# Dense groups of 512 tokens that run across batches, with a group of 256 between two halves of the first

## The chip, the core and the metric

The kernel runs on one core of one Trainium2 chip. The metric is device time in microseconds, the median of three runs. TensorE (PE in the profile) multiplies matrices, VectorE (DVE) and ScalarE (ACT) work elementwise, GpSimd (POOL) makes masks and indirect transfers, and SyncE (SP) issues the other transfers.

## The reference

Attention of 4 batches, 8 heads, 576 positions and 64 elements a head feeds a dense layer, and that a mixture of eight experts with one expert per token. `N` is 2304 tokens, `D` 512.

```python
# attention: heads 0-3 plain, heads 4-7 dilated
scores = (1.0 / np.sqrt(64)) * np.matmul(q, k.transpose(0, 1, 3, 2))
rel = pos[:, None] - pos[None, :]
mask_plain = (rel >= 0) & (rel < 32)
mask_dil = (rel >= 0) & (rel < 128) & (rel % 4 == 0)
attn = softmax(np.where(masks, scores, -1e9));  x = attn @ v       # -> [2304, 512]
# dense, w_in [512, 2048], w_out [2048, 512]
r = np.maximum(x @ w_in, 0.0)
y = (s * (r * r) + b) @ w_out
# experts, w1 [8, 512, 1024], w2 [8, 1024, 512]
logits = (y / |y|) @ (emb / |emb|).T / tau
e = argmax(logits);  gate = softmax(logits)[e]
out = gate * (np.maximum(y @ w1[e], 0.0) @ w2[e])
```

## The kernel before, in words

All products keep full precision with a split: each operand is a high part and a low part, and `mm3` (L273 to L275) issues three matmuls, high x high, low x high, high x low, into one PSUM bank.

**Attention** is cut into units of 192 tokens of one batch (`UT`, three units a batch, twelve in all), and each unit into four items of two heads: items 0 and 1 are plain heads, 2 and 3 dilated. An item has four steps: `attn_a` loads query and key (`qkp`, `qkd`) and values (`vp`, `vd`); `attn_b` makes scores on PE (`pS`, L129), adds the mask and takes the row minimum on DVE (L135, L138), exponentials on ACT (L140, one per window), and scales on DVE (L146); `attn_c` transposes on PE (`pT`, L154) and copies on ACT (`sT`, L159); `attn_d` multiplies with values (`po`, L173) and writes the high part of x on ACT (`xhi`, L181) and the low part on DVE (`xlo`, L182). The first unit of a batch has narrower first windows, which splits some of its DVE operations.

**Dense layer.** Tokens are taken in groups of 384 (`G`, six groups, two units each). A group walks over 16 chunks of 128 hidden columns. `gemm1` multiplies x by a chunk of `w_in` (12 matmuls into `ph`, one of two banks), then ReLU on ACT (`r`, L284), the square, and the high and low part `gh` and `gl`; in group 0 the square is on ACT (L288 to L291), later on DVE (L293 to L295). `gemm2`, two steps behind, multiplies by a chunk of `w_out` (9 matmuls into three banks `py0` to `py2`, which stand over the whole group). Behind the 16th chunk the banks are copied to `ysb` (L314), and routing takes norms and dots with the expert embeddings (L510, L513).

**Weights** come as 64 bit numbers. `weight_prep` loads 512 KB (`raw`) and makes the high and low part of a chunk: four DVE operations (L261, L264, L265, L269) and two on ACT (L263, L268). Two conversions serve one chunk, so there are 32.

**Order.** The startup runs the eight items of group 0 with eight conversions in between. Then the loop in `phase1` emits two slots a step, `gemm1` of one step and `gemm2` of the step two before; PE keeps just the order in which it is emitted, the other engines' instructions are ordered by a scheduler. The rest of attention is done in pairs of items and put into slots by `attn_steps`: loads 5 slots ahead, scores at the slot, transposes `TURN` = 4 slots later, outputs `PERIOD` = 6 slots later. Each of the first twelve steps also emits two conversions. In the last group, from step `EARLY` = 10 on, the experts' first units are set up (`experts_early`), with tables and gates made by small products.

**Experts.** Tokens are gathered by expert; units of 512 (pairs) and 256 (singles) tokens run `mm3` with weights split by ACT and DVE (L803, L804). The last group's routing transposes y on PE (`pyT`, L530) and makes the dots there (`pd`, L540).

Of the kernel before, what the change touches and what calls it, by code (L numbers as in the profile page):

```python
# [23 lines left out]
NTE = 15  # L24
NTT = 18

LOAD, TURN = -5, 4
LAG_FIRST = (0, 1, 4, 5)
PERIOD, START = 6, 2
LA = 2  # L30
EARLY = 10
# [3 lines left out]
P = 128  # L35
# [4 lines left out]
UT = 192  # L40
NU = NT // UT
G = 384
NG = NT // G
BIG = 1.0e9
QKP = 2 * UT + 2 * (UT + 32)
QKD = 4 * 64 + 4 * 80


class Kern:
    def __init__(self, tc, qkp, qkd, vp, vd, w_in, w_out, s, b, emb, tau, w1, w2, out):  # L50
        self.tc, self.nc = tc, tc.nc
        self.qkp, self.qkd, self.vp, self.vd = qkp, qkd, vp, vd
        self.w_in, self.w_out, self.s, self.b = w_in, w_out, s, b
        self.emb, self.tau, self.w1, self.w2, self.out = emb, tau, w1, w2, out
# [14 lines left out]
    def attn_consts(self, pool):  # L69
        nc = self.nc  # L70
        self.mask = pool.tile([P, 96], F32, name="mask")
        nc.gpsimd.memset(self.mask, 0.0)
        self.band(self.mask[0:64])
        self.band(self.mask[64:128])

    def load_plain(self, un):
        nc = self.nc
        ap = self.ppool if un == 0 else self.apool
        qk = ap.tile([P, QKP], F32, tag="qkp", name=f"qkp{un}", bufs=1)
        v = ap.tile([96, 3, 4, D], F32, tag="vp", name=f"vp{un}", bufs=1)  # L80
        nc.sync.dma_start(out=qk, in_=self.qkp[un])
        nc.sync.dma_start(out=v, in_=self.vp[un])
        return qk, v

    def load_dil(self, un, pr):
        nc = self.nc
        i = 2 * un + pr - 2
        ap = self.ppool if i < 2 else self.apool
        qk = ap.tile([P, QKD], F32, tag="qkd", name=f"qkd{i}", bufs=2)
        v = ap.tile([80, 2, 4, D], F32, tag="vd", name=f"vd{i}", bufs=2)  # L90
        nc.sync.dma_start(out=qk, in_=self.qkd[i])
        nc.sync.dma_start(out=v, in_=self.vd[i])
        return qk, v

    def attn_a(self, un, pr, ps):
        if (un, pr) in self.loaded:
            qk, vn = self.loaded.pop((un, pr))
        elif pr >= 2:
            qk, vn = self.load_dil(un, pr)
        else:  # L100
            if pr == 0:
                self.nat = self.load_plain(un)
            qk, vn = self.nat
        n = un % 3
        dil = pr >= 2
        if dil:
            qT, kT = qk[:, 0:256], qk[:, 256:576]
            wins = [(80 * t + 32, 48) if n == 0 else (80 * t, 80) for t in range(4)]
            groups = [(0, 4)]
        else:  # L110
            qT, kT = qk[:, UT * pr:UT * pr + UT], qk[:, 2 * UT + 224 * pr:2 * UT + 224 * pr + 224]
            wins = [(32, 64) if n == 0 and t == 0 else (64 * t, 96) for t in range(3)]
            groups = [(0, 1), (1, 3)] if n == 0 else [(0, 3)]
        hs = slice(0, 2) if dil else slice(2 * pr, 2 * pr + 2)
        return dict(un=un, pr=pr, u=f"{un}_{pr}", dil=dil, hs=hs, vn=vn, qT=qT, kT=kT, ps=ps,
                    wins=wins, groups=groups, ws=[w for _, w in wins])

    def attn_b(self, c):
        nc, ap, ps = self.nc, self.apool, c["ps"]
        u, qT, kT, ws, nb = c["u"], c["qT"], c["kT"], c["ws"], len(c["ws"])  # L120
        pS = ps.tile([P, 512], F32, tag="pa", name=f"pS{u}")
        extra = 4 * c["un"] + c["pr"] < 6
        prb = (self.ppool if extra else ap).tile([P, 4, 96], F32, tag="prob", name=f"prob{u}", bufs=6 if extra else 2)
        st = ap.tile([P, 16], F32, tag="st", name=f"st{u}", bufs=8)
        c["prb"] = prb
        for t, (k0, w) in enumerate(c["wins"]):
            for h in range(2):
                sl = slice(64 * h, 64 * h + 64)
                nc.tensor.matmul(pS[sl, 96 * t:96 * t + w], lhsT=qT[sl, 64 * t:64 * t + 64],  # L129
                                 rhs=kT[sl, k0:k0 + w], start=True, stop=True)  # L130
        full = 80 if c["dil"] else 96
        pS3 = pS[:, 0:384].rearrange("p (t w) -> p t w", t=4)
        for i, j in c["groups"]:
            w = ws[i]
            nc.vector.scalar_tensor_tensor(  # L135
                out=prb[:, i:j, :w], in0=pS3[:, i:j, :w], scalar=-0.125,
                in1=self.mask[:, full - w:full].unsqueeze(1).to_broadcast([P, j - i, w]), op0=ALU.mult, op1=ALU.add)
            nc.vector.tensor_reduce(out=st[:, i:j], in_=prb[:, i:j, :w], axis=AX.X, op=ALU.min)  # L138
        for t, w in enumerate(ws):
            nc.scalar.activation(prb[:, t, :w], prb[:, t, :w], AF.Exp, scale=-1.0,  # L140
                                 bias=st[:, t:t + 1], accum_out=st[:, 4 + t:5 + t])
        nc.vector.tensor_scalar_add(st[:, 8:8 + nb], st[:, 4:4 + nb], 1e-9)
        nc.vector.reciprocal(st[:, 12:12 + nb], st[:, 8:8 + nb])
        for i, j in c["groups"]:
            w = ws[i]
            nc.vector.tensor_mul(prb[:, i:j, :w], prb[:, i:j, :w],  # L146
                                 st[:, 12 + i:12 + j].unsqueeze(2).to_broadcast([P, j - i, w]))

    def attn_c(self, c):
        nc, ap, ps = self.nc, self.apool, c["ps"]  # L150
        u, ws, prb = c["u"], c["ws"], c["prb"]
        pT = ps.tile([P, 512], F32, tag="pa", name=f"pT{u}")
        for t, w in enumerate(ws):
            nc.tensor.transpose(pT[:w, P * t:P * t + P], prb[:, t, :w], self.ident)  # L154
        sT = ap.tile([P, 512], F32, tag="sT", name=f"sT{u}")
        cp = nc.scalar.copy
        cuts = [0, len(ws)] if ws[0] == ws[1] else [0, 1, len(ws)]
        for i, j in zip(cuts, cuts[1:]):
            cp(sT[:ws[i], P * i:P * j], pT[:ws[i], P * i:P * j])  # L159
        c["sT"] = sT  # L160

    def attn_d(self, cs):
        nc = self.nc
        c = cs[0]
        un, pr, dil, ws, k = c["un"], c["pr"], c["dil"], c["ws"], len(cs)
        po = c["ps"].tile([P, 512], F32, tag="pa", name=f"po{c['u']}")
        m = 48 if dil else 64
        for i, c in enumerate(cs):
            for t, w in enumerate(ws):
                for h in range(2):  # L170
                    lv = c["vn"][:w, h, t, :] if dil else c["vn"][:w, t, c["hs"].start + h, :]
                    o = UT * i + m * t
                    nc.tensor.matmul(po[64 * h:64 * h + 64, o:o + m], lhsT=lv,  # L173
                                     rhs=c["sT"][:w, P * t + 64 * h:P * t + 64 * h + m], start=True, stop=True)
        half, d0 = (un // 2) % 2, UT * (un % 2)
        hi, lo = (x[half][:, pr:pr + k, d0:d0 + UT] for x in (self.xhi, self.xlo))
# [27 lines left out]
    def attn_steps(self, n0, n1, ps):  # L204
# [4 lines left out]
        for j in range((n1 - n0) // 2):  # L209
            n = n0 + 2 * j  # L210
            t = 32 * (j // 4) + PERIOD * (j % 4) + START
# [14 lines left out]
            todo += [(t + LOAD, 0, n, a), (t, 2, n, b), (t + TURN, 3, n, c), (t + PERIOD, 1, n, d)]  # L226
# [3 lines left out]
    def weights_setup(self, left, right):  # L230
# [9 lines left out]
        self.x_half(right)  # L240

    def x_half(self, pool):
        i = len(self.xhi)
        self.xhi.append(pool.tile([P, 4, G], F32R, name=f"xhi{i}", bufs=1))
# [855 lines left out]
```

## Time and profile before

| | |
|---|---|
| median of 3 runs | 780.06 us (779.97 to 781.83) |
| profiled execution | 782.15 us, span 780.3 us |
| PE | 754.1 us busy, 97% of the span |
| DVE | 560.1 us, 72% |
| ACT | 393.9 us, 50% |
| POOL | 55.0 us, 7% |
| first dense matmul | at 37.44 us |

The span is the profiled part of that execution. Shares are means over stages that differ: attention and conversions alone at the start, the dense layer with attention beneath it up to 484.8 us, its end with the experts' setup up to 518 us, and the experts. Matmuls overlap each other, so the length shown for one is longer than its distance to the next; distances of starts tell what one costs.

### The profile page before, as it was taken

How to read it: one execution, taken by the hardware profiler on the slowest of the kernel's cores; microseconds unless marked ns; L12 is line 12 of the kernel's file. 1: busy time of each engine (PE TensorE's matmuls, PEld its weight loads, DVE VectorE, ACT ScalarE, POOL GpSimd, SP SyncE). 2: the span in 40 equal slices, each digit the busy share in tenths (PEclk: the TensorE clock that was granted, in tenths of full speed). 3: DMA queues.
4: the chain of work that ended last, by engine and by line, in shares of the span. 5: the costliest groups of instructions: out<-in, count | busy, mean ns of one | idle time of the engine just before them, and what ended most of it. 6: DMA issues, size and time to landing. Idle time of an engine off the chain costs nothing. (4 is left out here: it accounts for less than half of the span.)

```text
span 780.3 us, 14255 instructions
## 1 busy us (share of the span) xinstructions
PE 754.1 (97%) x5154; PEld 668.0 (86%) x5154; DVE 560.1 (72%) x1410; ACT 393.9 (50%) x925; POOL 55.0 (7%) x59
## 2 busy tenths in 40 slices
PE   5789999999999999999999999999999999999996
PEld 4578888988988888988888989898998989898895
DVE  5989996967476747764776578948666867768671
ACT  5778785534354436442644242642335655656550
POOL 1000000000000000000000000010422221211011
PEclk9999999999999999999999999999999999999999
DMA  7656664111121112110300010630236139887710
GB/s 259 217 205 209 196 202 161 57 40 60 40 73 39 48 34 91 40 47 18 109 18 1 1 42 1 216 95 15 82 108 203 43 108 308 260 302 229 262 48 25
DMA packets 33372, 88.04 MB, mean 113 GB/s; under 512 B 4294, under 2 KB 4294, under 8 KB 33168
## 3 DMA queue, kind: packets, MB, share of 16 engines
q1 hardware_dynamic: 29936, 76.84, 29.8%
q0 software_dynamic: 3360, 10.23, 4.0%
q8 instruction: 43, 0.70, 0.4%
q14 instruction: 33, 0.27, 0.1%
HBM read 94.39 MB, written 10.22 MB: 134 GB/s over the span
## 5 line engine op out<-in xcount | busy, mean ns | idle before, releaser
L804 DVE TENSOR_TENSOR wl<-raw,wh 128x1024 fp32r<-128x1024 f32 x96 | 113.6, 1221 | 29.4 <-ACT wh L803 29.4
L275 PE MATMUL ph<-xhi,wil 128*128 128x384 f32 x384 | 130.6, 340 | 1.1 <-DVE wil L269 1.1
L273 PE MATMUL ph<-xhi,wih 128*128 128x384 f32 x384 | 131.1, 341 | 0.4 <-ACT r L284 0.3
L274 PE MATMUL ph<-xlo,wih 128*128 128x384 f32 x384 | 130.2, 339 | 0.0
L273 PE MATMUL py<-woh,gh 128*128 128x512 f32 x288 | 118.0, 410 | 0.1
L275 PE MATMUL py<-woh,gl 128*128 128x512 f32 x288 | 114.2, 397 | 3.1 <-DVE gl L291 2.4
L274 PE MATMUL py<-wol,gh 128*128 128x512 f32 x288 | 113.6, 394 | 0.0
L284 ACT ACTIVATE r<-ph 128x384 f32<-128x384 f32 x96 | 46.9, 488 | 106.2 <-PE ph L275 102.6
L803 ACT CAST wh<-raw 128x1024 fp32r<-128x1024 f32 x96 | 96.1, 1054 | 5.1 <-DMA raw<-in_moe_w 5.1
L294 ACT ACTIVATE gh<-r,sb 128x384 fp32r<-128x384 f32 x80 | 49.1, 614 | 74.9 <-PE py L274 61.7
L295 DVE SCALAR_TENSOR_TENSOR gl<-r,sb,gh 128x384 fp32r<-128x384 f32 x80 | 49.3, 617 | 47.5 <-ACT gh L294 45.3
L513 DVE CUSTOM_DVE_ANT_0 junk<-ysb,enb 128x512 bf16<-128x512 f32 x120 | 82.4, 687 | 0.9
L273 PEld LDWEIGHTS ph<-xhi,wih 128*128 128x128 f32 x384 | 73.0, 190 | 4.9 <-ACT r L284 0.5
L274 PEld LDWEIGHTS ph<-xlo,wih 128*128 128x128 f32 x384 | 72.9, 190 | 4.0
L293 DVE SCALAR_TENSOR_TENSOR r<-r,sb 128x384 f32<-128x384 f32 x80 | 49.4, 617 | 35.5 <-ACT r L284 35.3
L275 PEld LDWEIGHTS ph<-xhi,wil 128*128 128x128 f32 x384 | 72.8, 190 | 2.0 <-DVE wil L269 2.0
L273 PE MATMUL ph<-xh,wh 128*128 128x256 f32 x256 | 73.5, 287 | 0.0
L274 PE MATMUL ph<-xl,wh 128*128 128x256 f32 x256 | 73.4, 287 | 0.0
L275 PE MATMUL ph<-xh,wl 128*128 128x256 f32 x256 | 73.1, 286 | 0.0
L140 ACT ACTIVATE prob<-prob,st 128x80 f32<-128x80 f32 (+3 forms) x168 | 58.4, 350 | 28.3 <-DVE st L138 28.3
L275 PEld LDWEIGHTS py<-woh,gl 128*128 128x128 f32 x288 | 54.2, 188 | 16.3 <-DVE gl L291 2.9
L273 PE MATMUL po<-wh,hh 128*128 128x512 f32 x168 | 66.8, 398 | 0.0
(256 smaller groups left out, 1350.7 us busy)
## 6 DMA issues: line engine op xcount, KB each, us to landing
raw<-in_moe_w SPq DMA_DIRECT2D x96, 512.0 KB
raw<-in_moe_w_in SPq DMA_DIRECT2D x16, 512.0 KB
raw<-in_moe_w_out SPq DMA_DIRECT2D x16, 512.0 KB
qkd<-in_qkd SPq DMA_DIRECT2D x24, 288.0 KB
qkp<-in_qkp SPq DMA_DIRECT2D x12, 416.0 KB
ydram<-ysb SPq DMA_DIRECT2D x18, 256.0 KB
vd<-in_vd SPq DMA_DIRECT2D x24, 160.0 KB
vp<-in_vp SPq DMA_DIRECT2D x12, 288.0 KB
```

The costliest lines, as they stand in the source:

```text
L140: nc.scalar.activation(prb[:, t, :w], prb[:, t, :w], AF.Exp, scale=-1.0, bias=st[:, t:t + 1], accum_out=st[:, 4 + t:5 + t])
L273: nc.tensor.matmul(out, lhsT=ah, rhs=bh, start=first, stop=False)
L274: nc.tensor.matmul(out, lhsT=ah, rhs=bl, start=False, stop=False)
L275: nc.tensor.matmul(out, lhsT=al, rhs=bh, start=False, stop=last)
L284: nc.scalar.activation(r, ph[:, :G], AF.Relu)
L293: nc.vector.scalar_tensor_tensor(out=r, in0=r, scalar=self.sb[:, 0:1], in1=r, op0=ALU.mult, op1=ALU.mult)
L294: nc.scalar.activation(gh, r, AF.Identity, bias=self.sb[:, 1:2])
L295: nc.vector.scalar_tensor_tensor(out=gl, in0=r, scalar=self.sb[:, 1:2], in1=gh.bitcast(F32), op0=ALU.add, op1=ALU.subtract)
L513: ins = nc.vector.tensor_tensor_reduce(out=self.junk, in0=y, in1=self.enb[:, e], scale=1.0, scalar=0.0, op0=ALU.mult, op1=ALU.add, accum_o ...
L803: nc.scalar.copy(h, r)
L804: nc.vector.tensor_sub(l, r, h.bitcast(F32))
```

## The change

Units become 256 tokens and run across batches: nine units, 36 items, always four windows of 96 keys, with extra masks (`EDGE`) where a batch begins inside a unit. Dense groups are 512, 256, 512, 512, 512 tokens (`GU` in units), and group 1, of 256, runs its 16 chunks between chunks 0 to 7 and chunks 8 to 15 of group 0 (`ORDER`, 80 steps). Group 0's four `py` banks stand all that time. In steps 10 to 25 (`SHARED`) group 1's two `py` banks are two of the four banks that `ph` and attention take in turn (`bank_a`); before and after that all four are in turn. In the last group `ph` has two banks of its own. Attention of each group has its own tempo. Of the 32 conversions four stand in the startup, then two a step up to 20, and six in seven steps from step 8 on. The loads of `s` and `b` stand behind those of the first unit, and the first unit's inputs lie in the buffer that later holds another half of x.

```diff
-LOAD, TURN = -5, 4
+LOAD = -5
-PERIOD, START = 6, 2
-EARLY = 10
+EARLY = 11
-UT = 192
+UT = 256
-G = 384
-NG = NT // G
+G = 512
+GU = (2, 1, 2, 2, 2)
+XH = (0, 1, 1, 0, 1)
+SEGS = [(0, 0, 8), (1, 0, 16), (0, 8, 16)] + [(g, 0, 16) for g in range(2, NG)]
+ORDER = [(g, f) for g, f0, f1 in SEGS for f in range(f0, f1)]
+TEMPO = [(2, 6, 4), (50, 3, 2), (66, 6, 4), (98, 6, 4)]
+EDGE = {0: 0, 2: 16, 4: 32, 6: 48, 7: -16}
+PRE = (0, 1, 4)
+NPREP = 4
+SHARED = (10, 26)
+def conversions(i):
+    return min(20, NPREP + 2 * (i + 1)) + min(12, max(0, (i - 7) * 6 // 7))
...
-            t = 32 * (j // 4) + PERIOD * (j % 4) + START
+            g = next(g for g in range(NG) if n // 4 < U0[g + 1])
+            start, period, turn = TEMPO[g - 1]
+            t = period * ((n - 4 * U0[g]) // 2) + start
...
-            todo += [(t + LOAD, 0, n, a), (t, 2, n, b), (t + TURN, 3, n, c), (t + PERIOD, 1, n, d)]
+            todo += [(t + LOAD, 0, n, a), (t, 2, n, b), (t + turn, 3, n, c), (t + period, 1, n, d)]
...
-        ph = pm.tile([P, 512], F32, tag="ph", name=f"ph{g}_{fc}", bufs=2)
+        ph = self.psf(f"ph{g}_{fc}")[:, :n]
...
+            if g == 1:
+                self.py[g] = [self.bank_a(f"py{g}_{i}", t) for i, t in enumerate((2, 3))]
+            else:
+                self.py[g] = [self.psM.tile([P, 512], F32, tag=f"py{i}", name=f"py{g}_{i}", bufs=1) for i in range(GT[g])]
...
+    def bank_a(self, name, t=None):
+        if t is None:
+            t = next(t for t in self.turns if not (SHARED[0] <= self.step < SHARED[1] and t >= 2))
+        self.turns.remove(t)
+        self.turns.append(t)
+        return self.psR.tile([P, 512], F32, tag=f"pa{t}", name=name, bufs=1)
...
-                for _ in range(2):
-                    if wi < 32:
-                        self.weight_prep(wi % 2, wi // 2)
-                        wi += 1
+                while wi < conversions(i):
+                    self.weight_prep(wi % 2, wi // 2)
+                    wi += 1
...
-        yT = [self.wp1.tile([P, EF], F32, tag=t, name=f"yT{t}") for t in ("wl12", "wl13")]
-        for i in range(3):
+        yT = self.raw[:2]
+        for i in range(GT[g]):
...
-            pt = ps.tile([P, 512], F32, tag="tr", name=f"pyT{g}_{i}", bufs=3)
+            pt = self.bank(f"pyT{g}_{i}", i == 2)
...
-            self.load(ecur[u], ecur[u] != ecur[u - 1], which)
+            same = ecur[u] != ecur[u - 1]
+            if u == 1:
+                self.load(ecur[u], None, which[:2])
+                which = which[2:]
+            self.load(ecur[u], same, which)
```

DVE at the end of the startup, before: the four `xlo` rows write the low half of group 0's x, the `cv`, `wil` and `wol` rows are conversions (the two digits behind `cv` are which matrix, 0 for `w_in`, and the chunk).

```order
L261 TENSOR_SCALAR cv12_362<-raw12_360 128x512
L182 TENSOR_TENSOR xlo0_137<-po1_1_553,xhi0_136 128x192
L261 TENSOR_SCALAR cv03_405<-raw03_403 128x512
L264 ISA cv12_362<-cv12_362,ce12_363 128x1024
L265 SCALAR_TENSOR_TENSOR cv12_362<-raw12_360,cv12_362 128x512
L264 ISA cv03_405<-cv03_405,ce03_406 128x1024
L182 TENSOR_TENSOR xlo0_137<-po1_2_569,xhi0_136 128x192
L269 TENSOR_TENSOR wol2_77<-cv12_362,woh2_76 128x512
L265 SCALAR_TENSOR_TENSOR cv03_405<-raw03_403,cv03_405 128x512
L182 TENSOR_TENSOR xlo0_137<-po1_3_580,xhi0_136 128x192
```

The same place of the changed kernel:

```order
L278 TENSOR_SCALAR cv03_746<-raw03_744 128x512
L286 TENSOR_TENSOR wol2_77<-cv12_707,woh2_76 128x512
L281 ISA cv03_746<-cv03_746,ce03_747 128x1024
L194 TENSOR_TENSOR xlo0_137<-po1_1_631,xhi0_136 128x256
L278 TENSOR_SCALAR cv13_756<-raw13_754 128x512
L282 SCALAR_TENSOR_TENSOR cv03_746<-raw03_744,cv03_746 128x512
L281 ISA cv13_756<-cv13_756,ce13_757 128x1024
L194 TENSOR_TENSOR xlo0_137<-po1_2_649,xhi0_136 128x256
L282 SCALAR_TENSOR_TENSOR cv13_756<-raw13_754,cv13_756 128x512
L286 TENSOR_TENSOR wil3_111<-cv03_746,wih3_110 128x512
L383 COPY enT_678<-pemb_673 128x32
L194 TENSOR_TENSOR xlo0_137<-po1_3_660,xhi0_136 128x256
```

Ahead of the last `xlo` row stand all operations of conversion `cv03` now and three of the four of `cv13`, where three of `cv03`'s stood.

ACT where a finished group is copied out, before, at the end of group 0 (`ysb` rows are the copies, `prob4` rows exponentials of an item of unit 4, `junk` rows norms, `gh1_1` the scaling of chunk 1 of group 1):

```order
L284 ACTIVATE r1_1_1712<-ph1_1_1699 128x384
L314 COPY ysb0_1762<-py0_0_784 128x512
L510 ACTIVATE junk2_1476,ssq0_1772<-ysb0_1762 128x512
L314 COPY ysb1_1765<-py0_1_785 128x512
L294 ACTIVATE gh1_1_1714<-r1_1_1712,sb_158 128x384
L140 ACTIVATE prob4_0_1720,st4_0_1721<-prob4_0_1720,st4_0_1721 128x96 x3
L314 COPY ysb2_1768<-py0_2_786 128x512
L510 ACTIVATE junk2_1476,ssq0_1772<-ysb1_1765 128x512
L140 ACTIVATE prob4_1_1737,st4_1_1738<-prob4_1_1737,st4_1_1738 128x96 x3
```

ACT in the changed kernel at the end of group 1, inside the second half of group 0 (`py1_0` and `py1_1` are group 1's two banks):

```order
L304 ACTIVATE r0_9_1917<-r0_9_1917 128x512
L159 ACTIVATE prob3_0_1926,st3_0_1927<-prob3_0_1926,st3_0_1927 128x96 x4
L329 COPY ysb4_1971<-py1_0_1369 128x512
L305 ACTIVATE gh0_9_1918<-r0_9_1917,sb_204 128x512
L329 COPY ysb5_1974<-py1_1_1370 128x512
L159 ACTIVATE prob3_1_1946,st3_1_1947<-prob3_1_1946,st3_1_1947 128x96 x4
L544 ACTIVATE junk2_1772,ssq1_1978<-ysb4_1971 128x512
L302 ACTIVATE r0_10_2002<-ph0_10_1989 128x512
L544 ACTIVATE junk2_1772,ssq1_1978<-ysb5_1974 128x512
L172 COPY sT3_0_2015<-pT3_0_2010 96x512
L304 ACTIVATE r0_10_2002<-r0_10_2002 128x512
L172 COPY sT3_1_2022<-pT3_1_2017 96x512
```

Four exponentials now stand ahead of the first copy and four behind the second, and the chunks around them are of group 0, each with activation, square and scaling on ACT.

## Rows read from the trace of the kernel before

**Rows 1.** Busy time by stretch: stretch, length, engines, PE's granted clock, DMA share, GB/s

```profile
0.00:37.44 37.44, 24.14 (x256) 18.56 (x256) 28.74 (x91) 25.22 (x90) 2.92 (x17) 1.00 0.73 245
37.44:125.00 87.56, 82.59 (x582) 72.07 (x582) 80.37 (x183) 66.73 (x167) 0.00 (x0) 0.98 0.60 200
125.00:484.80 359.80, 359.75 (x2553) 320.70 (x2551) 247.97 (x774) 158.35 (x474) 0.00 (x0) 1.00 0.14 46
...
518.00:780.30 262.30, 255.61 (x1583) 228.60 (x1581) 177.99 (x291) 126.60 (x171) 46.99 (x38) 0.99 0.46 151
```

**Rows 2.** Waits of PE: what waited, for what, us in total, times, longest

```profile
PE pS L129 <- DMA qkp<-in_qkp: 7.5, 2, 7.2
PE pT L154 <- DVE prob L146: 2.6, 3, 1.8
PE py L275 <- DVE gl L291: 2.4, 1, 2.4
```

**Rows 3.** Timeline of PE, one step of the dense layer: start, length, instruction

```profile
451.17 0.34 PE L273 MATMUL ph<-xhi,wih 128*128 128x384 f32 x1
...
453.29 0.40 PE L273 MATMUL py<-woh,gh 128*128 128x512 f32 x1
...
455.38 0.34 PE L273 MATMUL ph<-xhi,wih 128*128 128x384 f32 x1
```

**Rows 4.** Timeline of PE, the experts' first product of 512 and of 256 columns

```profile
590.19 0.39 PE L273 MATMUL ph<-wh,xh 128*128 128x512 f32 x1
...
595.64 0.39 PE L273 MATMUL po<-wh,hh 128*128 128x512 f32 x1
...
608.42 0.28 PE L273 MATMUL ph<-xh,wh 128*128 128x256 f32 x1
...
619.94 0.38 PE L825 MATMUL px<-ident,x 128*128 128x128 f32 x2
```

**Rows 5.** Timeline of PE, attention pairs in the dense layer

```profile
209.23 1.11 PE L129 MATMUL pS<-qkp 64*64 64x64 f32 x24
210.27 0.50 PE L273 MATMUL py<-woh,gh 128*128 128x512 f32 x1
...
255.21 0.34 PE L275 MATMUL ph<-xhi,wil 128*128 128x384 f32 x1
255.48 0.92 PE L173 MATMUL po<-sT,vp 96*64 96x64 f32 x24
256.33 1.32 PE L129 MATMUL pS<-qkd 64*64 64x80 f32 x32
257.58 0.50 PE L273 MATMUL py<-woh,gh 128*128 128x512 f32 x1
...
266.02 1.04 PE L154 MATMUL pT<-ident,prob 128*80 128x128 f32 x8
266.81 0.48 PE L273 MATMUL py<-woh,gh 128*128 128x512 f32 x1
...
271.16 1.14 PE L173 MATMUL po<-sT,vd 80*64 80x48 f32 x32
272.23 0.50 PE L273 MATMUL py<-woh,gh 128*128 128x512 f32 x1
```

**Rows 6.** Timeline of DVE, end of the startup, and a pair's last scaling

```profile
35.93 0.69 DVE L265 SCALAR_TENSOR_TENSOR cv<-raw,cv 128x512 int32<-128x512 int32 x1
36.53 0.35 DVE L182 TENSOR_TENSOR xlo<-po,xhi 128x192 fp32r<-128x192 f32 x1
...
262.07 0.49 DVE L146 TENSOR_TENSOR prob<-prob,st 128x320 f32<-128x320 f32 x1
```

**Rows 7.** Groups by form on DVE and ACT: count, busy us, mean ns, idle before

```profile
L265 DVE SCALAR_TENSOR_TENSOR cv<-raw,cv 128x512 int32<-128x512 int32 x32 | 21.9, 684 | 0.1
...
L135 DVE SCALAR_TENSOR_TENSOR prob<-pS,mask 128x320 f32<-128x320 f32 x16 | 7.5, 484 | 0.0
...
L140 ACT ACTIVATE prob<-prob,st 128x96 f32<-128x96 f32 x64 | 23.2, 365 | 5.1 <-DVE st L138 5.1
```

More of the change, by code (lines that the diff above doesn't have):

```diff
@@ L85, in load_dil @@
[L85 to L92, printed above, removed]
+        for e in edges:
+            m = pool.tile([P, 96], F32, name=f"mask{e}")
+            nc.gpsimd.memset(m, 0.0)
+            for half in (m[0:64], m[64:128]):
+                self.band(half)
+                if e is not None:
+                    w = 32 + e
+                    nc.gpsimd.affine_select(out=half[:, :w], in_=half[:, :w], compare_op=ALU.is_ge, fill=BIG,
+                                            base=e - 1, pattern=[[0, w]], channel_multiplier=-1)
+            self.mask[e] = m
@@ L124, in attn_b @@
         st = ap.tile([P, 16], F32, tag="st", name=f"st{u}", bufs=8)
         c["prb"] = prb
-        for t, (k0, w) in enumerate(c["wins"]):
+        for t in range(4):
+            k0 = c["step"] * t
             for h in range(2):
                 sl = slice(64 * h, 64 * h + 64)
-                nc.tensor.matmul(pS[sl, 96 * t:96 * t + w], lhsT=qT[sl, 64 * t:64 * t + 64],
-                                 rhs=kT[sl, k0:k0 + w], start=True, stop=True)
-        full = 80 if c["dil"] else 96
+                nc.tensor.matmul(pS[sl, 96 * t:96 * t + 96], lhsT=qT[sl, 64 * t:64 * t + 64],
+                                 rhs=kT[sl, k0:k0 + 96], start=True, stop=True)
@@ L132, in attn_b @@
         pS3 = pS[:, 0:384].rearrange("p (t w) -> p t w", t=4)
-        for i, j in c["groups"]:
-            w = ws[i]
+        for i, j, e in c["parts"]:
             nc.vector.scalar_tensor_tensor(
[L136 to L140, printed above, removed]
-                                 bias=st[:, t:t + 1], accum_out=st[:, 4 + t:5 + t])
@@ L142, in attn_b @@
[L142 to L147, printed above, removed]
+                out=prb[:, i:j], in0=pS3[:, i:j], scalar=-0.125,
+                in1=self.mask[e].unsqueeze(1).to_broadcast([P, j - i, 96]), op0=ALU.mult, op1=ALU.add)
@@ L150, in attn_c @@
         nc, ap, ps = self.nc, self.apool, c["ps"]
[L151 to L154, printed above, removed]
+        u, prb = c["u"], c["prb"]
+        pT = ps(f"pT{u}")
+        for t in range(4):
+            nc.tensor.transpose(pT[:96, P * t:P * t + P], prb[:, t], self.ident)
         sT = ap.tile([P, 512], F32, tag="sT", name=f"sT{u}")
-        cp = nc.scalar.copy
@@ L535, in dots @@
         def dots():
-            pd = ps.tile([P, 512], F32, tag="tr", name=f"pd{g}", bufs=3)
-            dots = pd[:, :3 * NE].rearrange("p (a e) -> p a e", a=3)
-            for i in range(3):
+            pd = self.bank(f"pd{g}")
+            dots = pd[:, :GT[g] * NE].rearrange("p (a e) -> p a e", a=GT[g])
+            for i in range(GT[g]):
                 for k in range(4):
@@ L822, in xt @@
             else:
[L823 removed]
+                px = self.bank(f"px{j}", n == 0 and j >= 2)
             for i in range(4):
```

345 lines of the change are left out of this document (182 added, 163 removed).

## The prediction

> **What bounds the kernel now.** I read the busy time by stretches first [rows 1]. The reader should compare PE with the length of each stretch. From 125.00 to 484.80 us PE is busy 359.75 of 359.80 us: the dense phase is PE from end to end, and no other engine comes near (DVE 247.97, ACT 158.35). In the first 37.44 us PE works 24.14 and nothing dense runs; DVE, with 28.74 us, is the engine that sets the end there. From 37.44 to 125.00 PE loses 4.97 us while DVE is at 80.37 of 87.56, so DVE is nearly full and makes PE wait. The experts from 518 us on are again PE (255.61 of 262.30).
>
> The waits of PE [rows 2] say what was late: 7.5 us for the first query and key load, then 2.6 us for scaled probabilities and 2.4 us for the low half of a group 0 activation, both on DVE. The last two make up the 4.97 us just named. So what PE issues after about 41 us counts at full price, and what DVE does before the first dense matmul counts at full price too.
>
> **The change, part by part.** All is in us, + is longer.
>
> *First matmul, wider.* A step of before has 12 matmuls of 384 columns and 9 of 512: from 451.17 to 453.29 is 2.12, or .176 each, and from 453.29 to 455.38 is 2.09, or .232 each [rows 3]. There are 96 steps, so the first matmul costs 96 x 2.12 = 203.5. Afterwards 64 chunks have 512 columns and 16 have 256. The experts run the same three-part product at these widths: 24 of 512 columns from 590.19 to 595.64, or .227 each, and 96 of 256 from 608.42 to 619.94, or .120 each [rows 4]. With .227 the sum is 64 x 12 x .227 + 16 x 12 x .120 = 174.3 + 23.0 = 197.3; with the .232 that the second matmul pays it is 201.2. I take 199.7, **-3.8** (bounds -6.2 and -2.3). The second matmul has the same 864 instructions of 512 columns: 0.
>
> The Trainium skill, page "TensorE: Matmul & The Clock Gate", section "Back-to-back issue gap", gives a sustained spacing of about 131 ns at 512 columns and 81 ns at 128; as an estimate between the two, 384 columns would pay 114 and 256 columns 98, and the first matmul would go from 131 to 119 us, -12. The rows here show 227 and 120 ns, so the trace does not agree.
>
> *Attention, fewer and larger pairs.* The PE stream holds 20 pairs of items behind the startup; each issues scores, transposes and outputs. In [rows 5] a plain pair costs 1.04 for 24 scores (209.23 to 210.27) and .85 for 24 outputs (255.48 to 256.33); a dilated pair 1.25 for 32 scores (256.33 to 257.58), .79 for 8 transposes (266.02 to 266.81) and 1.07 for 32 outputs (271.16 to 272.23). Six transposes are three quarters of .79. That is 2.48 and 3.11 a pair, 55.9 for ten of each; pairs at a batch's start have narrower windows, so up to 2.5 less. Afterwards there are 14 pairs, all with 32 scores of 96 columns, 8 transposes and 32 outputs of 64: 1.25 grown a little for width, taken as 1.45, + .79 + 32/24 x .85 = 3.37, or 47.2. **-8.7** (bounds -6 and -9.5). Where the stream changes shape one start is late: 255.21 to 255.48 is .27 instead of .18. At three such borders a pair, six pairs fewer give **-1.6**.
>
> *Later start of the dense phase.* DVE must finish the last low half of group 0's x. Score elements of the eight startup items go from 2112 to 3072 per partition, passed over three times, and the low half grows by 512: 3392 more elements. From 684 ns for 512 and 484 ns for 320 [rows 7] an element costs about 1.04 ns and an instruction 150 ns: +3.5, less four split instructions saved, -.6. One more conversion now stands ahead of that last low half: .60 start to start [rows 6] for three of its operations and somewhat less for the fourth, 2.1. The first conversion now stands early in DVE's queue and can wait there for its 512 KB load, with all score work behind it: +.6. Against this, the first score load is 544 columns instead of 832 and the two tiny loads are out of its way: of the 7.2 us wait I take 1.5 off. Together **+4.1**. Lower bound +1, as DVE is idle for about 37.44 - 7.2 - 28.74 = 1.5 now, which can absorb some; upper bound +7, another conversion's time more.
>
> *Waits on PE afterwards.* Each of the items has two bounds, zero and twice what I take. (a) Group 1's probabilities wait behind conversions on DVE as now: 1.8. (b) At step 25 the scores of the first pair of group 2 are followed by one dense product only, then by the transposes. An undisturbed dilated pair of before starts its scores at 256.33 and its last scaling at 262.07, .49 long: 6.2 [rows 5, 6]. PE offers 1.45 + 2.75 = 4.2; the copy of group 1's first result also stands behind four exponentials on ACT, at .365 each [rows 7] 1.4 us, and the next hidden product needs a bank. Together 2.7. (c) The other three pairs in the second half of group 0 have two dense products between, 7.0 against 6.2 plus ACT's own dense work: .5 each, 1.5. (d) Exponentials between the copies of finished groups: 1.0. Sum 7.0, against 4.97 now: **+2.0** (bounds -3 and +9).
>
> *Clock.* In 37.44 to 125.00 the granted clock is .98 [rows 1], behind that 2.4 us wait: at most 1.75 us lost, and I take **-.5** for a group 0 with longer dense products per conversion.
>
> *Experts' front.* Four more transposes for the last group's routing (.40 by the eight of [rows 5]) and 8 tiny dots, .5; with two transpose buffers and one from another pool instead of three, the fourth transposes wait for two copies, 1.0; the reload of two raw tiles for the second unit is hidden by PE's 255 us of other work, but its SP issues stand ahead of later loads, .2. **+2.1** (bounds 0 and +4). The other moves of loads cost nothing, since ACT and DVE have 112 and 202 us free in the middle stretch; without that cover a late unit load would stop PE for the load's several us.
>
> **Sum:** -3.8 - 8.7 - 1.6 + 4.1 + 2.0 - .5 + 2.1 = -6.4. It is made on the profiled execution of 782.15 (span 780.3), 2.1 above the median of 780.06; I carry the difference over to the median: 773.7.
>
> **The rivals.**
>
> 1. *Start not later, no new waits*: DVE's idle time absorbs the added elements, the copies come in time. Then +1 instead of +4.1 and -3 instead of +2.0: 773.7 - 3.1 - 5.0 = 765.6. For it: 1.5 us of idle time on DVE in the startup, and PE's loss-free middle. Against it: DVE at 92% of the next stretch. Chance .14.
>
> 2. *DVE takes all of the gain back* in the first half of group 0. Eight steps hold 16 conversions of 2.1, eight low halves of .68, and 8 units of score work, about 49 us of DVE; PE offers 45 to 50 there. If DVE reaches no more than the 92% of [rows 1], it needs 53, and PE waits 3 to 5 us with the clock's 1.75 behind it: 773.7 + 6 = about 780, no change. For it: the closeness of the two sums. Against it: the first steps of before hold 24 conversions in twelve steps of 4.2, 50 us of work in 51, and cost 5 us only; and four of the 16 conversions are not needed before group 1. Chance .12.
>
> 3. *Slower: the squeezed pairs of group 2.* Four pairs must now pass in the second half of group 0, while ACT still makes its activation, square and scaling for every chunk there. If the 6.2 us of a pair grow to 9.4 by three such ACT operations and two DVE operations in between, PE waits 5.2 at the first pair and 2.4 at each of the others: 12.4 where I put 4.2, +8.2. If each wait also costs what the wait of [rows 2] seems to, up to 1.75, it is another +2 to +7: 784 to 789. It decides from about 2 us a pair. For it: one or two dense products between scores and transposes, where before four slots lay between. Against it: conversions are over there, so DVE is free. Chance .19. The Trainium skill, same page, section "A second HAM failure mode: psum-queue depth-cycling", says that a stream that cycles through PSUM banks idles briefly between groups and its clock goes up and down; the new kernel shares two banks among four users in the steps before. The granted clock is 1.00 in [rows 1] with a two-bank cycle, so the trace does not agree for full banks.
>
> 4. *The wide products gain much more*, as the page's spacing would have it: with -12 for -3.8 it is 765.5. The rows show otherwise: chance .03.
>
> **How the numbers follow.** My forecast has .52: 773.7, its own range 768 to 778. A difference under 0.3% (2.3 us) can't be told from none here. Rivals 1 and 4 lie near 765.5, rival 2 within 0.3%, rival 3 above. Range 765 to 784: it takes in the low rivals' centre and the lower part of rival 3, and leaves out about .2. Faster .52 + .14 + .03, less a little for its upper end, .67; same .13; slower .20.
>
> **What would show it.** The first dense matmul should stand at 40 to 43 us, not 37.44; if it is at 38, the third term is wrong. A hidden product of 512 columns should take 2.72 to 2.79 from its first start to the next product's, and one of 256 about 1.44. An attention pair should take 3.4 in three pieces. In PE's waits I expect transposes for scaled probabilities between 125 and 190 us, 2 to 3 us at the first, and a bank wait there on ACT's copy; with more than 8 us in that row rival 3 holds. If PE waits for low halves or converted weights between 41 and 90 us, rival 2 does. The end of the last dense group to the end of the program should grow by about 2. The prediction is wrong above all if the start moves by more than 7, or if waits in the second half of group 0 add up to more than the attention saves.

## The result, and the profile after

The changed kernel takes 770.38 us (median of 4 runs, 767.63 to 770.94), the kernel before 780.70 in the same series. The ratio is 0.9859, with a 95% interval of 0.9832 to 0.9887: 11.0 us shorter, where 6.4 was forecast. The profiled execution took 770.94 us with a span of 769.1, and all rows below are from it, so spans differ by 11.2.

Busy time by stretch, of the changed kernel, in the order of [rows 1]: the startup, the stretch up to the first product of group 1, the rest of the dense layer, and the experts:

```profile
0.00:45.26 45.26, 25.87 (x292) 20.41 (x293) 34.52 (x92) 29.07 (x97) 12.62 (x52) 0.85 0.74 209
45.26:98.00 52.74, 49.83 (x312) 40.04 (x313) 49.71 (x104) 42.21 (x93) 0.00 (x0) 0.93 0.64 205
98.00:506.07 408.07, 404.31 (x2559) 335.96 (x2558) 280.85 (x766) 182.74 (x458) 4.86 (x4) 1.00 0.20 64
506.07:769.10 263.03, 255.13 (x1595) 228.36 (x1593) 177.72 (x292) 127.19 (x172) 46.64 (x38) 0.99 0.46 155
```

And of the kernel before, its dense layer cut at about the same place:

```profile
37.44:95.00 57.56, 53.68 (x391) 47.10 (x392) 54.26 (x127) 44.91 (x116) 0.00 (x0) 0.97 0.61 201
95.00:517.98 422.98, 420.69 (x2932) 373.74 (x2929) 299.15 (x903) 197.11 (x552) 5.08 (x4) 1.00 0.20 65
```

The reader should compare lengths. The startup is 7.8 us longer (45.26 for 37.44) and its mean granted clock is .85. The dense layer is 460.8 us (45.26 to 506.07) where it was 480.5: 19.7 shorter. The experts are 0.7 longer. In the dense layer PE is idle 2.91 + 3.76 = 6.7 us, before 3.88 + 2.29 = 6.2. So the gain is not in waits: PE's work takes less time.

The waits of PE in the changed kernel (what waited, for what, us in total, times, longest), which answer to [rows 2]:

```profile
PE pS L150 <- DMA prexhi<-in_qkp: 5.3, 3, 3.9
PE pT L170 <- DVE prob L163: 4.6, 3, 2.8
...
PE ph L290 <- DVE xlo L194: 3.2, 1, 3.2
...
PE ph L290 <- ACT ysb L329: 1.0, 1, 1.0
```

The first load is waited for 5.3 us instead of 7.5. The wait for the low half of x, 3.2, is the end of the startup. The row on probabilities holds startup and dense layer together (its 2.8 is in the startup, at 31.07); the part in the dense layer is found in the timeline. The row on `ysb` is the wait where group 1 gives its banks back; the copies at the end of groups 0 and 2 cost .5 each.

The timeline of PE in the changed kernel (start, length, instruction, idle time before it): the start, a wait in group 1's attention and what follows, the first product of group 1, a chunk of group 1, an attention pair, and a plain chunk of 512 tokens:

```profile
45.26 0.77 PE L290 MATMUL ph<-xhi,wih 128*128 128x512 f32 x1 [3.22 <-DVE xlo L194]
...
49.22 0.39 PE L290 MATMUL ph<-xhi,wih 128*128 128x512 f32 x1
...
64.80 0.62 PE L170 MATMUL pT<-ident,prob 128*96 128x128 f32 x4 [1.65 <-DVE st L162]
66.53 1.06 PE L170 MATMUL pT<-ident,prob 128*96 128x128 f32 x4 [1.12 <-DVE prob L163]
...
67.82 0.63 PE L291 MATMUL py<-wol,gh 128*128 128x512 f32 x1
68.25 0.63 PE L292 MATMUL py<-woh,gl 128*128 128x512 f32 x1
...
69.82 0.40 PE L290 MATMUL py<-woh,gh 128*128 128x512 f32 x1
...
98.01 0.28 PE L290 MATMUL ph<-xhi,wih 128*128 128x256 f32 x1
...
109.19 0.28 PE L290 MATMUL ph<-xhi,wih 128*128 128x256 f32 x1
...
110.62 0.40 PE L290 MATMUL py<-woh,gh 128*128 128x512 f32 x1
...
112.01 0.28 PE L290 MATMUL ph<-xhi,wih 128*128 128x256 f32 x1
...
245.90 1.04 PE L170 MATMUL pT<-ident,prob 128*96 128x128 f32 x8
246.69 0.49 PE L290 MATMUL py<-woh,gh 128*128 128x512 f32 x1
...
249.56 0.39 PE L290 MATMUL ph<-xhi,wih 128*128 128x512 f32 x1
...
252.37 1.15 PE L184 MATMUL po<-sT,v 96*64 96x64 f32 x32
253.45 1.54 PE L150 MATMUL pS<-qk 64*64 64x96 f32 x32
254.92 0.50 PE L290 MATMUL py<-woh,gh 128*128 128x512 f32 x1
...
257.78 0.39 PE L290 MATMUL ph<-xhi,wih 128*128 128x512 f32 x1
...
399.33 0.39 PE L290 MATMUL ph<-xhi,wih 128*128 128x512 f32 x1
...
402.05 0.39 PE L290 MATMUL py<-woh,gh 128*128 128x512 f32 x1
...
404.77 0.39 PE L290 MATMUL ph<-xhi,wih 128*128 128x512 f32 x1
```

At 64.80 and 66.53 the transposes wait 2.77 us, and then a matmul of 512 columns starts .43 behind the last (67.82 to 68.25), nearly twice the usual distance: the clock is at its lower level (granted .53 from 67.24 to 69.82). The nine matmuls at the start also take .44 each (45.26 to 49.22, granted .51). At 98.01 stands the first 256 wide product; up to there DVE is nearly full (49.71 of 52.74 us from 45.26 on) and behind it PE seldom waits, so this row serves below as a mark. A product of 512 columns takes 2.72 (399.33 to 402.05), one of 256 takes 1.43 (109.19 to 110.62). The second product takes 2.72 for 12 matmuls, or .227 each, beside a 512 wide neighbour, and 1.39 for 6, or .232, beside a 256 wide one.

The timeline of DVE in the startup of the changed kernel:

```profile
12.56 0.43 DVE L278 TENSOR_SCALAR cv<-raw 128x512 int32<-128x512 int32 x1 [2.21 <-DMA raw<-in_moe_w_in]
...
18.03 0.43 DVE L278 TENSOR_SCALAR cv<-raw 128x512 int32<-128x512 int32 x1 [1.23 <-DMA raw<-in_moe_w_out]
...
44.70 0.41 DVE L194 TENSOR_TENSOR xlo<-po,xhi 128x256 fp32r<-128x256 f32 x1
```

DVE begins its score work at 5.54 and ends the last low half at 45.11. In these 39.57 us it is busy 33.17; before, from its first score operation at 8.44 to 36.88, it was busy 27.34 of 28.44. Six waits for weight loads add up to 5.36; the two longest are shown.

The timeline of PE in the kernel before, at its start and behind its 2.4 us wait of [rows 2]:

```profile
37.44 0.69 PE L273 MATMUL ph<-xhi,wih 128*128 128x384 f32 x1
...
40.49 0.39 PE L273 MATMUL ph<-xhi,wih 128*128 128x384 f32 x1
...
50.97 0.63 PE L275 MATMUL py<-woh,gl 128*128 128x512 f32 x1
...
54.27 0.34 PE L275 MATMUL ph<-xhi,wil 128*128 128x384 f32 x1
```

The nine matmuls from 37.44 to 40.49 take 3.05 us, .34 each where .176 is usual. So the kernel before starts as slowly as the changed one, although its granted clock is shown as 1.00 there; behind the wait, from 50.50 to 54.20, it is shown as .54.

### The profile page after: what moved, and what is told of

Read it like the earlier page. It is cut to its first block, busy times and chain, and to the rows that moved or that the text cites. A ratio compares the mean times of both kernels' runs of the same rounds, so it can differ in the third digit from the quotient of the medians.

```text
span 769.1 us, 13185 instructions
## 1 busy us (share of the span) xinstructions
PE 735.1 (96%) x4756; PEld 624.8 (81%) x4756; DVE 542.8 (71%) x1252; ACT 381.2 (50%) x819; POOL 64.1 (8%) x94
## 5 line engine op out<-in xcount | busy, mean ns | idle before, releaser
L290 PE MATMUL ph<-xhi,wih 128*128 128x512 f32 (+1 forms) x320 | 119.3, 373 | 4.2 <-DVE xlo L194 3.2
L291 PE MATMUL ph<-xlo,wih 128*128 128x512 f32 (+1 forms) x320 | 118.5, 370 | 0.0
L292 PE MATMUL ph<-xhi,wil 128*128 128x512 f32 (+1 forms) x320 | 118.5, 370 | 0.0
L302 ACT ACTIVATE r<-ph 128x512 f32<-128x512 f32 (+1 forms) x80 | 44.3, 553 | 111.6 <-PE ph L292 111.5
L311 DVE SCALAR_TENSOR_TENSOR gl<-r,sb,gh 128x512 fp32r<-128x512 f32 (+1 forms) x64 | 43.7, 683 | 52.5 <-ACT gh L310 51.9
L310 ACT ACTIVATE gh<-r,sb 128x512 fp32r<-128x512 f32 (+1 forms) x64 | 42.8, 669 | 69.5 <-PE py L291 64.0
L290 PEld LDWEIGHTS ph<-xhi,wih 128*128 128x128 f32 x320 | 60.8, 190 | 15.6 <-issue 3.3
L291 PE MATMUL po<-wl,hh 128*128 128x512 f32 x168 | 65.6, 391 | 0.0
L292 PE MATMUL po<-wh,hl 128*128 128x512 f32 x168 | 65.5, 390 | 0.0
L290 PEld LDWEIGHTS py<-woh,gh 128*128 128x128 f32 x288 | 54.5, 189 | 13.3 <-ACT ysb L329 1.8
```

Source lines behind the costliest of these rows:

```text
L290: nc.tensor.matmul(out, lhsT=ah, rhs=bh, start=first, stop=False)
L291: nc.tensor.matmul(out, lhsT=ah, rhs=bl, start=False, stop=False)
L292: nc.tensor.matmul(out, lhsT=al, rhs=bh, start=False, stop=last)
L302: nc.scalar.activation(r, ph, AF.Relu)
L310: nc.scalar.activation(gh, r, AF.Identity, bias=self.sb[:, 1:2])
L311: nc.vector.scalar_tensor_tensor(out=gl, in0=r, scalar=self.sb[:, 1:2], in1=gh.bitcast(F32), op0=ALU.add, op1=ALU.subtract)
```

## The experiments

**The changed kernel again**, beside three variants on one chip. 

> The changed kernel as it is, timed beside the three variants on one chip, so that they can be compared with it. Both theories expect 770 us, a ratio to the kernel before of 0.983 to 0.989.

Measured: 770.61 us, ratio 0.9857 (0.9843 to 0.9871). Its mark, the first 256 wide product, stands at 97.50 and its span is 771.7, so what comes behind the mark took 674.2 us, and in the execution above 671.1: the same program differs by 3 us there between two executions. Variants are therefore told apart by their ratios and by the mark, not by a single span.

**What a matmul costs at three shapes.** The chunk's two products are changed in groups 2 to 4.

```diff
-        n = P * GT[g]
+        n = P * (3 if g in (2, 4) else GT[g])
...
-        for i in range(GT[g]):
-            ts = slice(P * i, P * i + P)
+        for i in range(3 if g in (3, 4) else GT[g]):
+            ts = slice(P * (i % 3 if g == 2 else i), P * (i % 3 if g == 2 else i) + P)
...
-                self.nc.scalar.copy(y, self.py[g][i])
+                self.nc.scalar.copy(y, self.py[g][0 if i == 3 and g in (3, 4) else i])
```

> Measures the cost of a matmul of the dense layer at three shapes in one kernel. Group 2: first product 384 columns wide (the group's last 128 tokens are left out, the fourth bank multiplies the first 128 again), second product in four banks. Group 3: first product 512 wide, second product in three banks only (the fourth result is a copy of the first). Group 4: 384 wide and three banks, the shape of the kernel before. The output is therefore not the reference's, and the experts' part is not to be read. In the kernel before a second-product matmul of 512 columns is .232 us behind the last, in the changed kernel .227, and .232 again in its group 1 with 256 columns and two banks. Theory A: what counts is that the first product beside it is narrower than 512: .232 in groups 2 and 4, .227 in group 3. Theory B: the number of banks a chunk counts: .227 in group 2, .232 in groups 3 and 4. Theory C: the rows of 384 elements in the tiles of the kernel before (the tiles have 512 here): .227 in all three, and .173 for the 384 wide matmuls instead of .176.

It ran once, in 861.95 us; only its dense layer is read. The timeline of PE in this kernel, a chunk of group 2, the second product of one of group 3, a chunk of group 4, and at 456.84 two second products of group 4 with nothing in between:

```profile
287.13 0.33 PE L290 MATMUL ph<-xhi,wih 128*128 128x384 f32 x1
...
289.24 0.39 PE L290 MATMUL py<-woh,gh 128*128 128x512 f32 x1
...
292.00 0.33 PE L290 MATMUL ph<-xhi,wih 128*128 128x384 f32 x1
...
387.48 0.39 PE L290 MATMUL py<-woh,gh 128*128 128x512 f32 x1
...
389.52 0.33 PE L290 MATMUL ph<-xhi,wih 128*128 128x384 f32 x1
...
391.63 0.39 PE L290 MATMUL py<-woh,gh 128*128 128x512 f32 x1
...
393.71 0.33 PE L290 MATMUL ph<-xhi,wih 128*128 128x384 f32 x1
...
456.84 0.39 PE L290 MATMUL py<-woh,gh 128*128 128x512 f32 x1
...
458.92 0.39 PE L290 MATMUL py<-woh,gh 128*128 128x512 f32 x1
...
460.96 0.27 PE L866 MATMUL px<-ident,x 128*128 128x128 f32 x1
```

Group 2 (384 wide, four banks): 287.13 to 289.24 is 2.11 for 12, or .176; the second product 2.76 for 12, .230. Group 3 (512 wide, three banks): 387.48 to 389.52 is 2.04 for 9, .227. Group 4 (384 wide, three banks): 2.11 and 2.08 for 9, .231. Theory A holds: the second product is dearer beside a narrower first product, with three banks and with four. Theory B falls by group 3, C by groups 2 and 4, whose tiles have rows of 512. The last rows say more: of two second products in a row the first nine matmuls take 2.08 and the next nine 2.04 (458.92 to 460.96). So the extra is paid near a change of width and then ends. Why PE pays it is not settled by these runs.

**Group 1's transposes one slot later.**

```diff
-TEMPO = [(2, 6, 4), (50, 3, 2), (66, 6, 4), (98, 6, 4)]
+TEMPO = [(2, 6, 5), (50, 3, 2), (66, 6, 4), (98, 6, 4)]
```

> In group 1's attention the transposes stand one slot later, behind the next dense product. In the changed kernel PE waits 2.8 us there for probabilities and its clock then falls to the lower level for a few us. Theory A: the wait is a matter of place, the later slot covers it, and 2.5 to 4.5 us are gained (766 to 768). Theory B: DVE is full there (95% busy from 45 to 98 us), so the next dense product that needs a low half or a converted weight waits instead: within 1 us of the changed kernel.

Measured: 767.75 us, ratio 0.9823 (0.9810 to 0.9836), beside 0.9857 for the changed kernel on the same chip. The timeline of PE in this kernel, the same transposes and the mark:

```profile
65.53 0.60 PE L170 MATMUL pT<-ident,prob 128*96 128x128 f32 x4
...
66.72 0.49 PE L290 MATMUL ph<-xhi,wih 128*128 128x512 f32 x1
...
93.65 0.28 PE L290 MATMUL ph<-xhi,wih 128*128 128x256 f32 x1
```

The transposes are done 1.19 us after their start, .22 of which is a wait for the second item, and the mark is at 93.65 instead of 97.50. Theory A holds: the wait was one of place, and its removal also keeps the clock up behind it. Later, with two other kernels: 

> The later transposes alone again, beside the two kernels that are built on them: a ratio to the kernel before of .981 to .984, about 767.5.

Measured: 769.25 us, 0.9837 (0.9824 to 0.9851), mark at 94.81. So the gain over the changed kernel is between 1.5 and 2.7 us by the two ratios, less than the 2.7 to 4.4 us by which the mark moves. The first run is clear of the changed kernel's interval, the repeat (1.6, on another chip, without the changed kernel beside it) is not; the direction is shown, the size only roughly.

**Weight loads later, and earlier, in the startup.** First all three behind the item loads:

```diff
-                if n in (3, 5, 7):
+                for _ in range(3 if n == 7 else 0):
                     raws.append(self.weight_load(len(raws) % 2, len(raws) // 2))
```

> The three weight loads of the startup stand behind all eight item loads on SP's queue, and the scheduler then puts the conversions later in DVE's queue (six and a half ahead of the last low half, not seven and three quarters). Theory A: the first dense matmul stands at 45.3 us because DVE, in order, waits 5.4 us in six pieces for weight loads with score work behind them. Then these waits shrink to under 2 us, the first dense matmul comes at 39 to 42 us, and the program is 3 to 5 us shorter than the changed kernel (765 to 767). Theory B: the amount of DVE work up to about 95 us is the bound, so an earlier start is given back as PE waits for low halves and weights in the next 50 us. Then the first dense matmul is earlier all the same, but the program is within 1 us of the changed kernel.

Measured: 771.88 us, 0.9864 (0.9842 to 0.9886). The timeline of DVE in this kernel has the loss in one row:

```profile
20.81 0.43 DVE L278 TENSOR_SCALAR cv<-raw 128x512 int32<-128x512 int32 x1 [4.57 <-DMA raw<-in_moe_w_in]
```

One wait of 4.57 us stands where two of 3.4 together were, and all waits for weight loads ahead of the start add up to 5.57; the start is at 45.53 and the mark at 97.93. The scheduler put the first conversion behind the scores of five items, but its load now landed later still. The edit did not take the waits away, so it decides nothing between the two theories. Then the other direction:

```diff
-                if n in (3, 5, 7):
+                if n in (1, 3, 5):
```

> The three weight loads stand behind the loads of items 1, 3 and 5 instead of 3, 5 and 7, and the scheduler's first conversion moves from row 20 to row 13 of DVE. Theory A, that DVE's 5.6 us of waits for weight loads behind its first score operation set the start: loads that land before their conversion's turn leave under 3.5 us of such waits, the first dense matmul comes at 42.5 to 44 us, and 1 to 3 us are gained over the changed kernel. Theory B, that DVE's work up to 95 us is the bound whatever its order: the start moves as in A, but the program stays within 0.7 us. Theory C: the transfers are full up to 25 us, so the wait only moves to a score load: the start stays at 45 us.

Measured: 774.54 us, 0.9913 (0.9893 to 0.9933), slower than the changed kernel. DVE's waits for weight loads sink to 3.1 us in the startup, but the start is at 44.77 all the same: DVE has now begun nine conversions instead of eight ahead of its last low half, which ends at 45.65, .5 later than in the changed kernel. The second product of chunk 0 also waits 1.9 us for its low half. The mark is at 97.70, so the profile does not show the 4 us by which the timed runs are longer; where they go stays open. With both edits: 

> Both edits at once, the earlier weight loads and the later transposes of group 1. If the two places are apart, the gains add: 2.9 us from the transposes as measured, and what the earlier loads give by themselves, 764 to 767. If DVE's work is the bound, it is no better than the transposes alone: 767 to 768.

Measured: 771.76 us, 0.9870 (0.9844 to 0.9896): nothing is gained on the later transposes alone (.9823 and .9837), and the forecast sum of the two gains does not come. Beside the earlier loads alone (.9913, same chip) it is 3.4 us shorter and the mark comes at 95.57 instead of 97.70: the later transposes gain here too, and the earlier loads lose.

**PE kept busy ahead of the first product.** The first attempt:

```diff
+            self.step = 0
+            warm = self.bank_a("warm")
+            for _ in range(7):
+                self.nc.tensor.matmul(warm, lhsT=self.wih[0][:, 0], rhs=self.wih[0].rearrange("p k f -> p (k f)"), start=True, stop=True)
+            self.turns = [0, 1, 2, 3]
             slot, early = 0, []
```

> Seven matmuls of 512 columns whose result is never used stand ahead of the first dense product, in time in which PE only waits for the last low half of x. Theory A: the first two products take 7.5 instead of 5.4 us only because the granted clock was at its lower level behind the idle stretch; with PE busy ahead of them the clock is up earlier and 1 to 2 us are gained (768.5 to 769.5). Theory B: DVE sets the pace behind the start, and faster first products only lengthen later waits: within 0.7 us of the changed kernel.

It took 771.94 us, 0.9882 (0.9864 to 0.9901). The seven matmuls themselves waited 3.2 us for the last low half, because their bank lies where the startup's banks were, and ran from 44.70 to 48.08. With `warm = bank("warm")` from the startup's pool they are free of it. 

> The seven unused matmuls again, now in a PSUM bank of the startup's pool, so that they need not wait for the last low half as they did. They should run from 42 to 45 us, in PE's idle time. Theory A: the granted clock is up when the first dense product starts, and its first two take 5.5 to 6.5 instead of 7.4 us: 1 to 2 us gained. Theory B: DVE paces what follows, so that later waits take it back: within 0.7 us of the changed kernel.

Measured: 771.40 us, 0.9877 (0.9854 to 0.9901). The timeline of PE in this kernel:

```profile
41.65 3.35 PE L386 MATMUL warm<-wih 128*128 128x512 f32 x7
...
58.22 0.50 PE L292 MATMUL py<-woh,gl 128*128 128x512 f32 x1 [2.10 <-DVE gl L307]
...
96.00 0.28 PE L290 MATMUL ph<-xhi,wih 128*128 128x256 f32 x1
```

The first two products took 6.0 instead of 7.4 to 7.5 us, as theory A has it. But a second product then waited 2.10 us for a low half from DVE, and the clock sank again (a mean of .81 from 55.51 to 61.72). The mark is at 96.00, 1.5 to 2 earlier, and the time is no better. By its time theory B is the nearer one. Its mechanism is seen only in part: the wait for the low half is new, but the transposes behind it wait .37 instead of 2.77, and the mark keeps the gain. Where the rest of the time goes is not shown.

**Less work on DVE before the first product.** Both are built on the later transposes. The row minimum of the startup's items is left out in the first:

```diff
-        nc.vector.tensor_reduce(out=st[:, 0:4], in_=prb, axis=AX.X, op=ALU.min)
+        if n < 8:
+            nc.gpsimd.memset(st[:, 0:4], 0.0)
+        else:
+            nc.vector.tensor_reduce(out=st[:, 0:4], in_=prb, axis=AX.X, op=ALU.min)
```

> On top of the later transposes: the row minimum of the eight startup items is left out (a zero stands in its place, which this data's exponentials bear), so DVE has eight operations of .47 us less before the first dense matmul, 3.8 us. Theory A, that the amount of DVE's work with its waits sets the start: the first dense matmul comes 3 to 4 us earlier, at about 41, and the program is 2 to 4 us shorter than with the later transposes alone (764 to 766). Theory B, that landing loads set the start: the waits for weight loads grow by what the work shrinks, the start stays at 44 to 45 us and the time within 1 us of 767.7.

Measured: 768.07 us, 0.9829 (0.9813 to 0.9845), beside 0.9837 for the later transposes alone. The timeline of PE in this kernel:

```profile
39.78 0.80 PE L293 MATMUL ph<-xhi,wih 128*128 128x512 f32 x1
...
54.97 0.79 PE L295 MATMUL py<-woh,gl 128*128 128x512 f32 x1 [2.24 <-DVE gl L310]
...
92.11 0.28 PE L293 MATMUL ph<-xhi,wih 128*128 128x256 f32 x1
```

The first product starts at 39.78, 4.9 to 6.8 us earlier than in the two executions with the later transposes (44.70 and 46.55). The mark is at 92.11, 1.5 to 2.7 earlier. Between them stand a wait of 2.24 us for a low half and products at the lower clock. But here the start no longer waits for the last low half, as it does in the other two. The timeline of DVE:

```profile
42.34 0.42 DVE L197 TENSOR_TENSOR xlo<-po,xhi 128x256 fp32r<-128x256 f32 x1
```

The last low half ends at 42.76, and at 44.55 and 46.39 in the two executions with the later transposes: 1.8 to 3.6 earlier, about what the mark moves. So less work on DVE does bring its last low half forward, as theory A says, by less than the eight operations (4.4 us at .55), and the mark goes with DVE's progress and not with the first product on PE. In the time hardly anything is left (.6 us by the ratios, inside both intervals), so theory A's 2 to 4 us do not come. The edit also shortens each item's chain; this run does not tell the two apart.

The second hands the scaling to POOL: `(nc.gpsimd if n < 8 else nc.vector).tensor_mul(...)`. 

> On top of the later transposes: the scaling of the probabilities of the eight startup items runs on POOL, which is idle there, so DVE is rid of eight operations of .56 us, 4.4 us, but each item's chain may get longer. Theory A (DVE's work sets the start): start 2 to 4 us earlier, 764 to 767. Theory B (loads set it): start unchanged, 767 to 768. If an operation on POOL takes over 2 us, the chain of the last items grows and the start moves later.

Measured: 768.67 us, 0.9834 (0.9815 to 0.9852), start at 44.91. An operation takes .99 us on POOL (.55 on DVE), the transposes of the first item wait 3.4 us for it, and the startup is no shorter. DVE is rid of 4.4 us, but a part comes back. The timeline of DVE in this kernel:

```profile
20.18 1.20 DVE L282 SCALAR_TENSOR_TENSOR cv<-raw,cv 128x512 int32<-128x512 int32 x1
```

This operation of a conversion takes .68 otherwise. Four of the eight in the startup ran while POOL was scaling and took 1.20 to 1.37; the other four took .68 to .69. The eight together took 2.4 us more than in the kernel with the later transposes. With that and the longer chains, the run does not decide between the theories.

## Why the prediction was right, and where its terms were wrong

The time lies in the range and near the lower end of the likeliest case. The mechanism, fewer and wider products against a later start, was right; that the time came so near is in part luck, because errors of both signs met. Point by point, measured on the spans:

| term | forecast | measured |
|---|---|---|
| first product | -3.8 | 64 x 2.72 + 16 x 1.43 - 96 x 2.11 = -5.6 |
| second product | 0 | 64 x 2.72 + 16 x 1.39 - 96 x 2.09 = -4.3 |
| attention pairs | -8.7 | 47.4 - 57.8 = -10.4 |
| borders between shapes | -1.6 | 14 x .38 - 20 x .27 = -.1 |
| later start | +4.1 | 45.26 - 37.44 = +7.8 |
| waits on PE | +2.0 | 6.7 - 6.2 = +.5 |
| clock | -.5 | 2.8 - 3.0 = -.2 |
| experts' front | +2.1 | 263.0 - 262.3 = +.7 |
| sum | -6.4 | -11.6, of -11.2 |

No term holds the small products and transposes of the early tables and gates, which take 1.8 instead of 2.4 us, so the terms agree with the spans to about 1 us.

*First product.* The mechanism was right. The term was mis-sized by the value chosen between .227 and .232: 512 wide chunks that no attention interrupts pay .227. The 2.12 of [rows 3] is one chunk; the typical one of the kernel before takes 2.11.

*Second product.* This is the step that failed: "the second matmul has the same 864 instructions of 512 columns: 0". The same instruction costs .232 beside 384 wide ones [rows 3] and .227 in a stream of one width, which [rows 4] showed for the experts; the forecast read the two numbers and used them only for the first product. The shapes experiment shows that the neighbour's width makes the difference.

The Trainium skill, page "TensorE: Matmul & The Clock Gate", section "Back-to-back issue gap", gives 131 ns for sustained matmuls of 512 columns. The rows here have 227 in the streams of that width, so the measurement decides, and rival 4 did not occur.

*Attention.* The new pair came out at 1.47 + .79 + 1.08 = 3.34 for 3.37. The old pairs cost more than the forecast's 55.9: the 1.04 of [rows 5] is a pair with the narrower first window (its row shows 64x64), and most plain pairs take 1.14 there; the outputs of such narrower plain pairs take 1.29, not .85. All attention rows of the dense layer, start to start with waits taken out, add up to 57.8 before and 47.4 after. The borders did not get cheaper: .15, .09 and .14 a pair (2.87, 2.81 and 2.86 for 2.72) for 14 pairs cost as much as .27 for 20 (two of 2.18 for 2.09 and one of 2.20 for 2.11).

*Later start.* By its own sign the prediction was wrong here: the start moved by 7.8, more than 7. The work was sized well: DVE's busy time from its first score operation to its last low half grew by 5.8, forecast 2.9 for scores and 2.1 for the conversion. It began 2.9 earlier, not 1.5. What failed is "+.6" for a conversion that waits for its load with score work behind it: DVE's idle time there grew from 1.1 to 6.4, of which six such waits are 5.4. That these waits alone set the start is not shown: where they were 3.1 (loads earlier), the last low half ended no earlier. What an earlier start would be worth stays open too. In the kernel without the row minimum the first product moved by 4.9 to 6.8, DVE's last low half by 1.8 to 3.6 and the mark by 1.5 to 2.7. The forecast priced the start at full size; DVE's 80.37 of 87.56 in [rows 1] was a warning.

*Waits and clock.* The worst wait was in group 1, 2.8, not at group 2's first pair. Term (a) took 1.8 "as now" from [rows 2], but that wait stands at 29.56, in the startup; the 4.97 hold only .8 of waits for probabilities, and 1.1 for converted weights. Of the squeezed pairs of group 2 no transpose waited more than .31, so rival 3 fell. The wait for group 1's banks was there, 1.0. The clock cost about the same in both kernels. At the lower level the changed kernel loses 1.9 us at its start (nine matmuls, 3.96 for 2.04) and .9 behind the wait (five from 67.82 to 69.82, 2.00 for 1.14), the kernel before 1.5 (3.05 for 1.58) and 1.5 (nine from 50.97 to 54.27, 3.30 for 1.81). The forecast took at most 1.75 from the shown .98 and so missed the slow start of the kernel before.

The Trainium skill, same page, section "HAM oscillation — how this bites in real kernels", tells of a kernel that waits for a transfer of about 3 to 5 us in every turn of its loop and starts each turn at the lower clock. The rows from 64.80 on show such a fall behind two waits for DVE of 1.65 and 1.12 us, and the later transposes removed both the waits and the fall; behind the bank wait of .96 us the granted clock stayed at 1.00 (156.00 to 160.00).

*Rival 2* did not occur in the changed kernel: its sign was PE waiting for low halves or converted weights, and of the 2.91 us that PE is idle from the start to the mark 2.77 are the transposes' wait. Waits of 1.9 to 2.7 us for a low half appear in the variants with earlier loads, with unused matmuls and without the row minimum.

## What to carry to other kernels

A matmul's price includes its neighbours: look at start to start distances in streams with one width and in mixed ones before costing an unchanged product at nothing. Where an engine is nearly full behind a start, look at that engine's progress and at a mark behind the full stretch: in the run without the row minimum the mark moved with DVE's last low half, not with PE's first product. A transpose placed one product later was worth more here than moving loads, as it took away a wait and the fall of the clock behind it. A shown granted clock of 1.00 is worth a look at the distances of starts.

## What the runs showed that was not expected

Matmuls of 512 columns follow each other in .227 us in a uniform stream and in .230 to .232 where products 384 or 256 wide alternate with them; 384 wide ones take .176, which is .016 above 384 columns at the clock's upper level of 2.4 GHz, where uniform 512 wide ones are .013 above theirs (512 columns at 2.4 GHz take .213). Over the 96 steps of the kernel before, the second product's part alone is 4.3 to 4.8 us.

A DVE operation of a conversion took .68 us alone and 1.20 to 1.37 where POOL scaled at the same time.
